# Down projection of seven pairs of token tiles by Strassen's scheme, with the tokens normalised ahead of gate and up

## The chip, the core and the metric

One core of one Trainium2 chip runs the kernel. Its engines work side by side, each through its own list of instructions: TensorE (PE: matrix products into PSUM; PEld: the loading of the stationary operand), VectorE (DVE), ScalarE (ACT), GpSimd (POOL) and SyncE (SP), which here issues the DMAs. The metric is the device time of one execution in microseconds (us). Traces and the profile's page come from one profiled execution.

## The reference

The input is x, 2048 tokens of 640 values. Two blocks follow each other, both with a layer norm in front and a residual sum behind.

```python
def _A_ref(x, wqkv, w_phi, wo):            # H = 32 heads of Dh = 20
    qkv = ((x @ wqkv).reshape(B, S, 3, H, Dh)).transpose(2, 0, 3, 1, 4)
    q, k, v = qkv[0], qkv[1], qkv[2]
    pq = jnp.einsum("bhsd,hdf->bhsf", q, w_phi)
    pk = jnp.einsum("bhsd,hdf->bhsf", k, w_phi)
    phi_q = jnp.concatenate([_softmax(pq), _softmax(-pq)], axis=-1)
    phi_k = jnp.concatenate([_softmax(pk), _softmax(-pk)], axis=-1)
    kv = jnp.einsum("bhsf,bhsd->bhfd", phi_k, v)
    ...
    return o.transpose(0, 2, 1, 3).reshape(B, S, D) @ wo

def _B_ref(x, w_gate, w_up, w_down):       # F = 1536
    h = (x @ w_gate) * (x @ w_up)
    return h @ w_down

h  = x + _A_ref(_layernorm(x), A_wqkv, A_w_phi, A_wo)
h2 = h + _B_ref(_layernorm(h), B_w_gate, B_w_up, B_w_down)
```

There is no nonlinearity between the norm and the product g * u, so the factor 1/std of a token, which enters both g and u, can be taken out and applied as 1/var after the down product.

## The kernel before

The 2048 tokens are 16 tiles of 128; four tiles make a block (b = 0 to 3), so that each block has 512 tokens. The work is written as units, and a unit's name says what it does to which tile: `k`, `v`, `q` are the projections with their exponentials; `K` and `Q` sum and normalise the features; `A` builds the state kv over all tiles; `n` is the product of the features with kv, `h` the output product of the attention with the residual sum (`watt`), `f b.ft.j` one 128-column slice ft of gate and up for block b (`fu`; block 0 is done in two halves, j = 0 and 2), and `d` and `e` the down product of a tile with the store (`fd`; the last block's four tiles have the name `e` for all but the first instruction).

The order of the instructions on each engine is not found while the program runs. It is a table, `ORDER`, with one string of unit names for each engine: the n-th time that a name stands there, the n-th instruction of that unit on that engine has its place. `Prog.place` walks these five lists, gives out the buffers of the pools (four PSUM buffers `ps` of two banks, two output buffers `outb`, two `gate`, and so on) as they come free by estimated times, and `Prog.finish` adds the waits on semaphores. The estimated times (`t`, `lat`) only decide which buffer is given to whom; each engine carries out its list strictly in order and waits where an operand or a buffer is missing.

The steps that the change touches:

- `watt(t)`: ten products on TensorE, of which the last column gives the mean of the attention's output. DVE adds the token's mean (`mh`, L1009), subtracts it from the sum and writes the residual `x_all` (L1012). The tile is turned by a DMA transpose issued by SP (L475) into `hT`, which gate and up read; tiles 0 and 1 are turned by TensorE. Beside this ACT sums the squares (L571), and POOL makes the variance and its inverse `rs` (L1018, L1020). `rs` is wanted only after the down product.
- `fu`: five matmuls of 512 columns for gate, five for up (256 in the halves of block 0). ACT copies gate out of PSUM (L1033), DVE multiplies it with up and writes `hhT` (L1035), which is the stationary operand of the down product. `hhT` and `hT` are double-buffered over the blocks and lie in the memory of the keys, which in the trace and below gives them the name `phik`; the weights of the down product, `Wd`, lie in that of the values and have the name `vaug`.
- `fd(t)`: 24 matmuls of 320 columns (12 slices of the hidden dimension, two halves of the output). For tiles 0 to 11 ACT scales the result and adds the mean (L1048), POOL adds the residual (L1051), SP stores 160 KB. For the last four tiles ACT adds the mean to the residual beforehand (L1058) and DVE does scaling and sum in one instruction (L1069); the last tile is cut into 512 and 128 columns (L1076), with a store for each.

All matrix products go through one helper, line L578 in the profile.

Of the kernel before, what the change touches and what calls it, by code (L numbers as in the profile page):

```python
# [1170 lines left out]
```

## Time and profile before

| | |
|---|---|
| median of 3 runs | 279.02 us (279.02 to 279.13) |
| profiled execution | 279.5 us, span of the trace 277.6 us |
| TensorE busy | 272.1 us, 98% of the span, granted clock 1.0 |
| DVE, ACT, POOL busy | 167.3, 141.6, 107.8 us |
| down product, 384 matmuls in all | group of 360 with 320 columns that the trace names: 50.4 us |

The chain that ended last is read from the end of the trace backwards: at each step to what released the instruction, or to the one before it on the same engine. A group in the list by lines has its busy time, the mean duration of one instruction, and the idle time before it with what ended that. The duration of a matmul is its time through the array, and matmuls overlap, so that their pace is read from a row of them and not from the mean of one. A few matmuls have no record.

### The profile page before, as it was taken

To read this page: it belongs to the slowest core of one execution; us is meant where nothing else is said; L and a number is where in the kernel's file an instruction comes from. 1 tells how busy PE (TensorE), PEld (TensorE's weight loads), DVE (VectorE), ACT (ScalarE), POOL (GpSimd) and SP (SyncE) were. 2 spreads that over 40 slices of the span, in tenths; PEclk is the share of its full clock that TensorE was granted. 3 is DMA by queue.
4 is the path that set the end of the run, shared out by engine and by line. 5 is a ranking of instruction groups with operands and counts; after the bars stand their busy time and mean duration, and the time that the engine had idled before them with its cause. 6 is when DMAs were issued, how large, how long until landed. Compare 5 with 4: busy or idle time off the path is not lost.

```text
span 277.6 us, 5581 instructions
## 1 busy us (share of the span) xinstructions
PE 272.1 (98%) x2258; PEld 185.0 (67%) x2271; DVE 167.3 (60%) x314; ACT 141.6 (51%) x249; POOL 107.8 (39%) x152
## 2 busy tenths in 40 slices
PE   8999999999999999999999999999999999999995
PEld 8777776777877888877746565565565444457773
DVE  1899999999998888667855652353400223331012
ACT  2469999999586873454354814212623414220330
POOL 5437999999822323302341419002334000100520
PEclk9999999999999999999999999999999999999999
DMA  8997989305575557986656322751130000000112
GB/s 189 285 144 165 147 269 399 143 2 86 139 103 106 92 132 138 300 104 87 124 128 72 59 47 50 151 73 24 24 97 24 24 2 0 0 0 2 71 48 72
DMA packets 67241, 28.60 MB, mean 103 GB/s; under 512 B 57744, under 2 KB 65936, under 8 KB 67216
## 3 DMA queue, kind: packets, MB, share of 16 engines
q1 hardware_dynamic: 66288, 27.90, 46.4%
q10 hardware_dynamic: 928, 0.35, 0.5%
q8 instruction: 18, 0.29, 0.4%
q14 instruction: 7, 0.06, 0.1%
HBM read 11.82 MB, written 2.62 MB: 52 GB/s over the span
## 4 chain that ended last, share of the span: by engine, by line
PE 83%; DVE 7%; POOL 4%; DMA 2%; issue 1%; SPq 1%
PE ps L578 82%; POOL phik L871 3%; DVE ps L846 2%; DMA Wp<-in_A_wqkv_dram 2%; DVE Sq L908 2%; DVE Ssum L868 2%; POOL eq L920 1%; SPq L475 1%; DVE Rk L870 1%; PE ps L486 0%; DVE outb L1076 0%; SPq L471 0%; DVE Phi L958 0%; DVE rq L914 0%; DVE nb L849 0%
## 5 line engine op out<-in xcount | busy, mean ns | idle before, releaser
L578 PE MATMUL ps<-phik,Wgu 128*128 128x512 bf16 (+1 forms) x588 | 106.0, 335 | 0.5
L578 PEld LDWEIGHTS ps<-phik,Wgu 128*128 128x128 bf16 x600 | 58.3, 98 | 42.9 <-DVE phik L1035 0.6
L578 PE MATMUL ps<-Wp,xT 128*128 128x320 bf16 (+1 forms) x480 | 69.6, 299 | 0.2 <-ACT phik L854 0.2
L1035 DVE TENSOR_TENSOR phik<-ps,gate 128x512 bf16<-128x512 f32 (+1 forms) x60 | 34.0, 580 | 55.6 <-PE ps L578 50.0
L1033 ACT ACTIVATE gate<-ps 128x512 bf16<-128x512 f32 (+1 forms) x60 | 30.2, 512 | 66.5 <-PE ps L578 50.9
L578 PE MATMUL ps<-vaug,phik 128*128 128x320 bf16 (+3 forms) x559 | 59.4, 265 | 0.2
L578 PEld LDWEIGHTS ps<-Wp,xT 128*128 128x128 bf16 x480 | 45.5, 98 | 17.7 <-ACT phik L854 0.5
L578 PEld LDWEIGHTS ps<-vaug,phik 128*128 128x128 bf16 x560 | 42.6, 98 | 16.2
L871 POOL TENSOR_TENSOR phik<-phik,Rk 128x1280 bf16<-128x1280 bf16 x16 | 37.5, 2361 | 3.4 <-DVE Rk L870 3.1
L1051 POOL TENSOR_TENSOR outb<-t,x_all 128x640 bf16<-128x640 f32 x12 | 16.7, 1399 | 56.1 <-ACT t L1048 56.1
L1048 ACT ACTIVATE t<-ps,mh,rs 128x640 f32<-128x640 f32 x12 | 10.6, 884 | 34.3 <-PE ps L578 24.8
L846 DVE TENSOR_REDUCE ps<-ps 128x1 f32<-128x640 f32 (+1 forms) x32 | 26.2, 821 | 2.7 <-PE ps L578 2.4
L915 POOL TENSOR_TENSOR rq<-Sq,rq 128x33 f32<-128x33 f32 x16 | 4.1, 256 | 58.4 <-DVE rq L914 52.7
L908 DVE TENSOR_REDUCE Sq<-eq 128x66 f32<-128x1320 bf16 x16 | 24.2, 1514 | 2.8 <-ACT eq L854 2.8
L868 DVE TENSOR_REDUCE Ssum<-phik 128x64 f32<-128x1280 bf16 x16 | 23.5, 1471 | 0.2 <-ACT phik L854 0.2
L920 POOL TENSOR_TENSOR eq<-eq,rq 128x660 bf16<-128x660 bf16 x16 | 20.9, 1306 | 0.9
L854 ACT ACTIVATE eq<-ps,nb,rs 128x300 bf16<-128x300 f32 (+2 forms) x26 | 17.0, 688 | 8.1 <-DVE nb L849 6.6
L571 ACT ACTIVATE junk<-x_all 128x640 bf16<-128x640 bf16 x20 | 14.7, 735 | 4.6 <-DVE x_all L1012 4.6
L854 ACT ACTIVATE eq<-ps,nb,nrs 128x300 bf16<-128x300 f32 (+2 forms) x26 | 16.9, 696 | 0.0
L854 ACT ACTIVATE phik<-ps,nb,rs 128x640 bf16<-128x640 f32 x16 | 14.2, 886 | 2.8 <-DVE nb L849 2.6
L1069 DVE SCALAR_TENSOR_TENSOR outb<-ps,rs,t 128x640 bf16<-128x640 f32 x3 | 2.7, 884 | 20.8 <-PE ps L578 18.0
L1018 POOL TENSOR_SCALAR vpe<-shc 128x1 f32<-128x1 f32 x16 | 3.1, 191 | 30.3 <-ACT junk L571 29.4
(86 smaller groups left out, 247.4 us busy)
## 6 DMA issues: line engine op xcount, KB each, us to landing
x_all<-in_A_x_dram SPq DMA_DIRECT2D x4, 640.0 KB, 5.1
out_dram<-outb SPq DMA_DIRECT2D x15, 160.0 KB, 1.8
Wgu<-in_B_w_gate_dram SPq DMA_DIRECT2D x1, 1920.0 KB, 11.3
Wgu<-in_B_w_up_dram SPq DMA_DIRECT2D x1, 1920.0 KB, 16.1
vaug<-in_B_w_down_dram SPq DMA_DIRECT2D x1, 1920.0 KB, 9.1
Wp<-in_A_wqkv_dram SPq DMA_DIRECT2D x1, 800.0 KB, 5.2
phiqT<-in_A_wqkv_dram SPq DMA_DIRECT2D x1, 800.0 KB, 6.6
Wo<-in_A_wo_dram SPq DMA_DIRECT2D x1, 800.0 KB, 7.0
```

Source lines behind the costliest of these rows:

```text
L571: g.op("ACT", lambda e: e.activation(out=junk[:, v.i, :], in_=in_, func=func, accum_out=acc), rd=rd, wr=wr, use=[v], t=0.73, lat=0.97)
L578: ins = e.matmul(o_, lhsT=l_, rhs=r_, start=s_, stop=p_, skip_group_check=True)
L846: g.op("DVE", lambda e: e.tensor_reduce(out=mx(), in_=src(), axis=AX.XY if len(src().shape) == 3 else AX.X, op=ALU.max, apply_absolute_val ...
L854: g.op("ACT", lambda e, s=s, sc=sc, to=to, of=of: e.activation(out=to(s), in_=of(), func=ACT.Exp, bias=nb[:, i:i + 1], scale=sc[:, t:t + 1 ...
L868: g.op("DVE", lambda e: e.tensor_reduce(out=Ssum[:, vs.i, :], in_=x, axis=AX.X, op=ALU.add), rd=R_phik[t], wr=vs.R, use=[vs], t=1.39, lat=1.5)
L871: g.op("POOL", lambda e: e.tensor_tensor(out=x, in0=x, in1=Rk[:, vr.i, :].unsqueeze(2).to_broadcast([P, 2 * H, DH]), op=ALU.mult), rd=vr.R ...
L908: g.op("DVE", lambda e: e.tensor_reduce(out=Sq[:, vs.i, :].rearrange("p (w g) -> p w g", w=NQ), in_=feat(0, NQ).rearrange("p w (g f) -> p ...
L920: return e.tensor_tensor(out=x, in0=x, in1=rq[:, vr.i, :].rearrange("p (w h) -> p w h", h=HW).unsqueeze(3).to_broadcast([P, NQ, HW, DH]), ...
L1033: g.op("ACT", lambda e: e.activation(out=gate[:, vg.i, 0:P * n], in_=PS[v.i][:, 0, 0:P * n], func=ACT.Copy), rd=[v.R[0]], wr=vg.R, use=[v, ...
L1035: g.op("DVE", lambda e: e.tensor_tensor(out=hhT[:, hb, ft, sl], in0=PS[v.i][:, 1, 0:P * n], in1=gate[:, vg.i, 0:P * n], op=ALU.mult), rd=[ ...
L1048: g.op("ACT", lambda e: e.activation(out=t32[:, v3.i, :].rearrange("p (b n) -> p b n", b=2), in_=PS[v.i][:, :, 0:HALF], func=ACT.Identity, ...
L1051: g.op("POOL", lambda e: e.tensor_tensor(out=outb[:, vo.i, :], in0=t32[:, v3.i, :], in1=x_all[:, t, :], op=ALU.add), rd=v3.R + [R_h[t]], w ...
```

## The change

Two things are changed together.

**The down product of a pair of tiles.** The two tiles of a pair are the two block rows of a 2x2 matrix whose block columns are the two halves of the hidden dimension (6 slices of 128 each); `w_down` is cut in the same way into 2x2 blocks of 768 x 320. Strassen's scheme computes the four blocks of the product from seven block products instead of eight, each of sums or differences of blocks. `weight_sums` makes the five sums of weight blocks (T0 to T4, 1920 values a partition) once, on POOL, in the memory of the projection weights `Wp` and of `xT`, which are no longer needed by then. `block_sums` makes the five sums of hidden blocks of a pair (S0 to S4, 768 values a partition) on DVE, in the memory of `xT`. `down_pair` has seven groups of six matmuls. Products that go into two results are copied out of PSUM by ACT as float32 (`snap`, L1161) while further products are added onto them in PSUM; POOL forms the sums of these copies and of the residual (`padd`, L1167, six a pair); DVE adds a sum to what stands in PSUM and writes the output tile (`fin`, L1172, four a pair). A pair takes two of the four PSUM buffers from its first product on. Tiles 0 and 1 (`RAW`) are multiplied as before (`down_raw`).

**The norm ahead of gate and up.** Since sums of two tiles' hidden blocks are formed, both must carry their own 1/std already. For tiles 2 to 15 `watt` now lets ACT sum the squares of h - mean, POOL take the power -1/2, and DVE write the normalised tile `hb` (L1062); the DMA transpose reads `hb`. Nothing has to be scaled after the down product. For tiles 0 and 1 the path stays.

The table `ORDER` is a new one from q2 on, on all engines. On SP two loads of x (`lx2`, `lx1`) stand ahead of the first transposes of the queries, and the load of `w_down` (`ld`) ahead of those of tile 4.

```diff
@@ -42,6 +42,7 @@
 SC = 175.0 / 128.0
+RAW = (0, 1)
...
-        "f3.0.0 f3.0.0 f2.1.0 f3.1.0 f3.11.0 f3.10.0 f3.11.0 f3.1.0 f2.5.0 f2.5.0 e12 d9 e12 d11 d8 e14 d10 e14 e13 e13 e15 e15",
+        "D3.0 D2.1 D3.0 D2.1 D2.1 D3.0 D3.0 D3.0 D3.1 D3.0 D3.1 D3.0 D3.1 D3.1 D3.1 D3.1 D3.1",
...
-    t32 = sb([P, 2, D], FP32, "t32")
+    t32 = sb([P, 2, HALF], FP32, "t32")
+    hb = sb([P, 2, D], BF16, "hb")
...
+    KH = NF // 2
+    xTf = xT[:, :, :, :].rearrange("p t c n -> p (t c n)")
+    eqf = eq[:, :, :].rearrange("p b n -> p (b n)").bitcast(FP32)
+    Wkv = Wp[:, :, D:3 * D]
+    TW = [Wkv[:, 0:3, 0:2 * HALF], Wkv[:, 0:3, 2 * HALF:4 * HALF], Wkv[:, 3:5, 0:3 * HALF],
+          xTf[:, 0:KH * HALF].rearrange("p (a n) -> p a n", a=3), xTf[:, KH * HALF:2 * KH * HALF].rearrange("p (a n) -> p a n", a=3)]
+    o1 = 2 * KH * HALF
+    SH = [[xTf[:, o1 + KH * P * (2 * k + i):o1 + KH * P * (2 * k + i + 1)].rearrange("p (f n) -> p f n", f=KH) for i in range(2)]
+          for k in range(5)]
...
-        g.op("DVE", lambda e: e.tensor_tensor(out=mh[:, t:t + 1], in0=PS[v.i][:, 1, HALF:HALF + 1], in1=mv[:, t:t + 1], op=ALU.add),
-             rd=v.R + [R_mv[t]], wr=[R_mh[t]], use=[v], t=0.11, lat=0.2)
+        if t in RAW:
...
         xv = x_all[:, t, :].rearrange("p (b n) -> p b n", b=2)
+        g.op("DVE", lambda e: e.tensor_tensor(out=xv, in0=PS[v.i][:, :, 0:HALF], in1=xv, op=ALU.add),
+             rd=v.R + [R_x[t // 4]], wr=[R_h[t]], use=[v], t=0.75, lat=0.87)
+        act_sum(x_all[:, t, :], ACT.Square, shc[:, t:t + 1], [R_h[t], R_nmh[t]], [R_shc[t]], bias=nmh[:, t:t + 1])
...
+        vh = Buf(p_hb)
+        g.op("DVE", lambda e: e.tensor_scalar(out=hb[:, vh.i, :], in0=x_all[:, t, :], scalar1=nmh[:, t:t + 1], scalar2=rs[:, i:i + 1],
+                                              op0=ALU.add, op1=ALU.mult), rd=[R_h[t], R_nmh[t], R_rs[i]], wr=vh.R, use=[vh],
+             t=0.27, lat=0.37)
+        turned(t, 1, lambda: hT[:, bb, :, P * tt:P * (tt + 1)], lambda: hb[:, vh.i, :], vh.R, [R_hT[bb][tt]], [vh])
...
+    def weight_sums():
+        lo, hi = (0, HALF), (HALF, D)
+        for k, (a, b, op) in enumerate(((0, 3, ALU.add), (1, 3, ALU.subtract), (2, 0, ALU.subtract), (0, 1, ALU.add), (2, 3, ALU.add))):
+            U("T%d" % k)
+
+            def part(q, n):
+                f0, (c0, c1) = KH * (q // 2), (lo, hi)[q % 2]
+                return Wd[:, f0:f0 + KH, c0:c1].rearrange("p (a w) n -> p a w n", w=n)
+
+            def out_(n, k=k):
+                return TW[k].rearrange("p a (w n) -> p a w n", w=n)
+            n = TW[k].shape[2] // HALF
+            pool_op(lambda e, a=a, b=b, op=op, n=n, part=part, out_=out_: e.tensor_tensor(out=out_(n), in0=part(a, n), in1=part(b, n), op=op),
+                    4.0, rd=[R_Wd], wr=[R_T[k]])
+
+    def block_sums(b, i):
+        hb_, c0 = b % 2, 2 * P * i
+
+        def part(q):
+            f0, c = KH * (q % 2), c0 + P * (q // 2)
+            return hhT[:, hb_, f0:f0 + KH, c:c + P]
+        for k, (x, y, op) in enumerate(((0, 3, ALU.add), (2, 3, ALU.add), (0, 1, ALU.add), (2, 0, ALU.subtract), (1, 3, ALU.subtract))):
+            U("S%d.%d.%d" % (b, i, k))
+            rd = [R_hhT[hb_][ft][2 * i + q // 2] for q in (x, y) for ft in range(KH * (q % 2), KH * (q % 2) + KH)]
+            g.op("DVE", lambda e, k=k, x=x, y=y, op=op: e.tensor_tensor(out=SH[k][i], in0=part(x), in1=part(y), op=op),
+                 rd=rd, wr=[R_S[k][i]], t=0.6, lat=0.72)
...
+        def mm(v, bk, l_, r_, first, more=()):
+            g.op("PE", lambda e: mms(e, [(PS[v.i][:, bk, 0:HALF], l_[0](ft), r_[0](ft), first and ft == 0, False) for ft in range(KH)]),
+                 rd=l_[1] + r_[1], wr=[v.R[bk]], use=[v] + list(more), t=0.815, lat=0.965)
+
+        def slot(x):
+            return eqf[:, HALF * x.i:HALF * (x.i + 1)] if x.i < 6 else t32[:, x.i - 6, :]
+
+        def snap(v, bk):
+            x = Buf(p_slot)
+            o = g.op("ACT", lambda e: e.activation(out=slot(x), in_=PS[v.i][:, bk, 0:HALF], func=ACT.Copy), rd=[v.R[bk]], wr=x.R,
+                     use=[v, x], after=SLOT_USERS, t=0.42, lat=0.55)
+            return x, o
+
+        def padd(o_, a, y, op=ALU.add, x=None):
+            r_, in1 = (y.R, lambda: slot(y)) if x is None else ([R_h[x[0]]], lambda: x_all[:, x[0], HALF * x[1]:HALF * (x[1] + 1)])
+            g.op("POOL", lambda e: e.tensor_tensor(out=slot(o_), in0=slot(a), in1=in1(), op=op), rd=a.R + r_, wr=o_.R,
+                 use=[o_, a] + ([y] if x is None else []), t=0.72)
+
+        def fin(v, bk, o_, t, y=None, after=()):
+            in1 = (lambda: slot(y)) if y is not None else (lambda: x_all[:, t, HALF * bk:HALF * (bk + 1)])
+            g.op("DVE", lambda e: e.tensor_tensor(out=outb[:, o_.i, HALF * bk:HALF * (bk + 1)], in0=PS[v.i][:, bk, 0:HALF], in1=in1(),
+                                                  op=ALU.add), rd=[v.R[bk], R_h[t]] + (y.R if y is not None else []), wr=[o_.R[bk]],
+                 use=[v, o_] + ([y] if y is not None else []), after=after, t=0.45, lat=0.57)
...
+        mm(v1, 1, summed(2), wraw(3), True, [v2])
+        s5, _ = snap(v1, 1)
+        mm(v2, 0, raw(3), wsum_(2), True)
+        s4, _ = snap(v2, 0)
+        mm(v1, 0, summed(0), wsum_(0), True)
+        s1, _ = snap(v1, 0)
+        mm(v1, 1, raw(0), wsum_(1), False)
+        c12, a12 = snap(v1, 1)
+        fin(v1, 1, o1_, t1, after=[a12])
+        mm(v2, 0, summed(1), wraw(0), False)
+        c21, a21 = snap(v2, 0)
+        fin(v2, 0, o2_, t2, after=[a21])
+        mm(v1, 0, summed(4), wsum_(4), False)
+        mm(v2, 1, summed(3), wsum_(3), True)
+        padd(s4, s4, s5, ALU.subtract)
+        padd(s5, s4, None, x=(t1, 0))
+        padd(s1, s1, s4)
+        padd(s1, s1, None, x=(t2, 1))
+        padd(s1, s1, c12)
+        padd(s1, s1, c21, ALU.subtract)
+        fin(v1, 0, o1_, t1, s5)
+        store(o1_, t1)
+        fin(v2, 1, o2_, t2, s1)
+        store(o2_, t2)
...
+    def down(b):
+        for i in range(2):
+            if 4 * b + 2 * i in RAW:
+                down_raw(4 * b + 2 * i)
+                down_raw(4 * b + 2 * i + 1)
+                continue
+            block_sums(b, i)
+            down_pair(b, i)
+
+    for b in range(2):
+        each(queries, b)
+        each(num, b)
+        each(watt, b)
+    each(queries, 2)
+    each(num, 2)
+    each(queries, 3)
+    g.alias(R_T, R_Wp[1] + R_Wp[2] + R_xT[0:6])
+    weight_sums()
+    g.alias([r for x in R_S for r in x], R_xT[5:])
+    ffn(0)
+    each(watt, 2)
+    each(num, 3)
+    ffn(1)
+    down(0)
+    ffn(2)
+    each(watt, 3)
+    down(1)
+    ffn(3)
+    down(2)
+    down(3)
```

What the new order is at three places follows. A row is a source line, operation, output and inputs by name, the shape, and the number of equal instructions in a row.

The end of TensorE's list: before, tiles 13 to 15, each 24 matmuls, the last tile in two parts.

```order
L578 MATMUL ps1<-vaug,phik 128x320 x24
L578 MATMUL ps0<-vaug,phik 128x320 x12
L578 MATMUL ps3<-vaug,phik 128x320 x24
L578 MATMUL ps0<-vaug,phik 128x320 x12
L578 MATMUL ps2<-vaug,phik 128x320 x24
L578 MATMUL ps1<-vaug,phik 128x512 x12
L578 MATMUL ps1<-vaug,phik 128x128 x12
```

In the change, the last two pairs; `xT` and `Wp` are the places of the sums (S, T3 and T4 in `xT`, T0 to T2 in `Wp`).

```order
L604 MATMUL ps0<-xT 128x320 x6
L604 MATMUL ps1<-vaug,xT 128x320 x6
L604 MATMUL ps2<-xT 128x320 x6
L604 MATMUL ps3<-vaug,xT 128x320 x6
L604 MATMUL ps1<-Wp,phik 128x320 x6
L604 MATMUL ps3<-xT 128x320 x6
L604 MATMUL ps2<-Wp,xT 128x320 x6
L604 MATMUL ps2<-Wp,phik 128x320 x6
L604 MATMUL ps1<-vaug,xT 128x320 x6
L604 MATMUL ps2<-xT 128x320 x6
L604 MATMUL ps1<-xT 128x320 x6
```

Three tiles' products have become groups of six that alternate between the pairs, each pair with two PSUM buffers, and the last product is added onto a buffer of which ACT has taken a copy.

The end of POOL's list: before, the residual sums of the last tiles that POOL serves (8 to 11).

```order
L1018 TENSOR_SCALAR vpe<-shc 128x1
L1020 TENSOR_TENSOR rs<-vpe,mone 128x1
L1051 TENSOR_TENSOR outb<-t32,x_all 128x640 x4
```

In the change, the six float32 sums of the last pair, of which the last is wanted for the last output.

```order
L1167 TENSOR_TENSOR t32<-t32,eq 128x320 x2
L1167 TENSOR_TENSOR eq<-eq,t32 128x320
L1167 TENSOR_TENSOR t32<-eq,x_all 128x320
L1167 TENSOR_TENSOR eq<-eq 128x320
L1167 TENSOR_TENSOR eq<-eq,x_all 128x320
L1167 TENSOR_TENSOR eq<-eq 128x320 x2
```

POOL had no part in the last four tiles; now it stands between their products and their outputs.

DVE ahead of block 2 of gate and up: before, the residual of a tile (`x_all`) is what the transpose reads.

```order
L1009 TENSOR_TENSOR mh<-ps3,mv 128x1
L1012 SCALAR_TENSOR_TENSOR x_all<-ps3,mh,x_all 128x640
L1035 TENSOR_TENSOR phik<-ps2,gate 128x512
L993 RECIPROCAL rden<-ps3 128x32
L1035 TENSOR_TENSOR phik<-ps0,gate 128x512
L995 TENSOR_TENSOR ob<-ps3,rden 128x640
```

In the change, the scaled tiles 8 and 9 (the two rows that write `hb`), around the eviction of tile 0's down product.

```order
L1019 RECIPROCAL rden<-ps0 128x32
L1021 TENSOR_TENSOR ob<-ps0,rden 128x640
L1062 TENSOR_SCALAR hb<-x_all,nmh,rs 128x640
L1125 SCALAR_TENSOR_TENSOR outb<-ps1,rs,x_all 128x640
L1062 TENSOR_SCALAR hb<-x_all,nmh,rs 128x640
L1110 TENSOR_TENSOR xT<-phik 128x768
L1019 RECIPROCAL rden<-ps0 128x32
```

The scaling is a further instruction between the residual sum and the transpose, and it has a place of its own in DVE's list, behind an attention tile (`ob`) and a down tile (`outb`).

More of the change, by code (lines that the diff above doesn't have):

```diff
@@ L230, in place @@
                 o = queue[e][head[e]]
-                if any(b.i is None and not b.pool.free for b in o.bufs):
+                want = {}
+                for b in o.bufs:
+                    if b.i is None:
+                        want[b.pool] = want.get(b.pool, 0) + 1
+                if any(len(p.free) < n for p, n in want.items()):
                     continue
@@ L418, in _build @@
     shc = sb([P, NT], FP32, "shc")
[L419 removed]
+    nmh = sb([P, NT], FP32, "nmh")
     mhalf = sb([P, 1], FP32, "mhalf")
@@ L452, in _build @@
     p_Ss, p_Rk, p_Sq, p_rq, p_rden = Pool(2), Pool(2), Pool(2), Pool(2), Pool(2)
+    p_hb, p_slot = Pool(2), Pool(8)
+    R_T, R_S = regs(5), [regs(2) for _ in range(5)]
+    SLOT_USERS = []
     R_x, R_h = regs(4), regs(NT)
@@ L1015, in watt @@
-        turned(t, 1, lambda: hT[:, bb, :, P * tt:P * (tt + 1)], lambda: x_all[:, t, :], [R_h[t]], [R_hT[bb][tt]], [])
-        act_sum(x_all[:, t, :], ACT.Square, shc[:, t:t + 1], [R_h[t]], [R_shc[t]])
+        if t in RAW:
+            g.op("DVE", lambda e: e.tensor_tensor(out=nmh[:, t:t + 1], in0=mv[:, t:t + 1], in1=PS[v.i][:, 1, HALF:HALF + 1], op=ALU.subtract),
+                 rd=v.R + [R_mv[t]], wr=[R_nmh[t]], use=[v], t=0.11, lat=0.2)
+            xv = x_all[:, t, :].rearrange("p (b n) -> p b n", b=2)
+            g.op("DVE", lambda e: e.scalar_tensor_tensor(out=xv, in0=PS[v.i][:, :, 0:HALF], scalar=nmh[:, t:t + 1], in1=xv,
+                                                         op0=ALU.subtract, op1=ALU.add),
+                 rd=v.R + [R_x[t // 4], R_nmh[t]], wr=[R_h[t]], use=[v], t=0.8, lat=0.92)
+            turned(t, 1, lambda: hT[:, bb, :, P * tt:P * (tt + 1)], lambda: x_all[:, t, :], [R_h[t]], [R_hT[bb][tt]], [])
+            act_sum(x_all[:, t, :], ACT.Square, shc[:, t:t + 1], [R_h[t]], [R_shc[t]])
+            i = NT + t
+            pool_op(lambda e: e.tensor_scalar(out=vpe[:, i:i + 1], in0=shc[:, t:t + 1], scalar1=1.0 / D, scalar2=EPS_LN,
+                                              op0=ALU.mult, op1=ALU.add), 0.2, rd=[R_shc[t]], wr=[R_vpe[i]])
+            pool_op(lambda e: e.tensor_tensor(out=rs[:, i:i + 1], in0=vpe[:, i:i + 1], in1=mone[:, 0:1], op=ALU.pow),
+                    0.55, rd=[R_vpe[i], R_const], wr=[R_rs[i]])
+            return
@@ new lines, in down_raw, with two @@
+    def down_raw(t):
+        U("d%d" % t)
+        b, col, i = t // 4, P * (t % 4), NT + t
+        v, vo = Buf(p_ps, 2), Buf(p_outb, 2)
+        g.op("ACT", lambda e: e.activation(out=x_all[:, t, :], in_=x_all[:, t, :], func=ACT.Identity, bias=nmh[:, t:t + 1]),
+             rd=[R_h[t], R_nmh[t]], wr=[R_h[t]], t=0.75, lat=0.83)
+        g.op("PE", lambda e: mms(e, [(PS[v.i][:, bk, 0:HALF], hhT[:, b % 2, ft, col:col + P], Wd[:, ft, HALF * bk:HALF * (bk + 1)],
+                                      ft == 0, ft == NF - 1) for ft in range(NF) for bk in range(2)]),
+             rd=[r[t % 4] for r in R_hhT[b % 2]] + [R_Wd], wr=v.R, use=[v], t=3.257, lat=3.41)
+        def two(x):
+            return x.rearrange("p (b n) -> p b n", b=2)
+        g.op("DVE", lambda e: e.scalar_tensor_tensor(out=two(outb[:, vo.i, :]), in0=PS[v.i][:, :, 0:HALF], scalar=rs[:, i:i + 1],
+                                                     in1=two(x_all[:, t, :]), op0=ALU.mult, op1=ALU.add),
+             rd=v.R + [R_h[t], R_rs[i]], wr=vo.R, use=[v, vo], t=0.8, lat=0.92)
+        g.op("SP", lambda e: e.dma_start(out[0, P * t:P * (t + 1), :], outb[:, vo.i, :]), rd=vo.R, use=[vo], dma=("out", 4),
+             t=0.6, lat=0.3, size=0.4)
@@ L1128, in _build, with each, ffn @@
     load(Wd[:, :, :], B_w_down.rearrange("(f p) n -> p f n", p=P), [R_Wd], 1.92)
-    for b in range(NB):
+    def each(f, b):
         for t in range(4 * b, 4 * b + 4):
-            queries(t)
-        for t in range(4 * b, 4 * b + 4):
-            num(t)
-        for t in range(4 * b, 4 * b + 4):
-            watt(t)
+            f(t)
+    def ffn(b):
         for j, n in SPLIT[b]:
@@ L1138, in _build @@
                 fu(b, ft, j, n)
-        for t in range(4 * b, 4 * b + 4):
-            fd(t)
+    def down(b):
[27 more added lines that the diff above has]
+    down(3)
     g.order = ORDER
```

91 lines of the change are left out of this document (34 added, 57 removed), and 76 rows, old and new, of the table ORDER.

## The prediction

> **What bounds the kernel now.** I read the page's busy times first, then the chain that ended last, then the groups by shape, and the timeline of the end.
>
> ```profile
> span 277.6 us, 5581 instructions
> PE 272.1 (98%) x2258; PEld 185.0 (67%) x2271; DVE 167.3 (60%) x314; ACT 141.6 (51%) x249; POOL 107.8 (39%) x152
> PEclk9999999999999999999999999999999999999999
> PE 83%; DVE 7%; POOL 4%; DMA 2%; issue 1%; SPq 1%
> ...
> 74.88 1.93 PE ps L578 x22
> ...
> 216.60 10.74 PE ps L578 x49
> ...
> 238.18 33.34 PE ps L578 x216
> ...
> 271.57 2.55 PE ps L578 x11
> 274.13 0.03 issue
> 274.15 1.02 DVE outb L1076 x2
> ```
>
> TensorE is busy for 272.1 of 277.6 us at the full granted clock, and from 83 us on the chain consists of its matmuls alone, up to the two evictions that begin at 274.15. Before that, DVE and POOL have a share of the chain (the keys, 40 to 75 us), but TensorE is full there too. So a matmul taken away is time gained, as long as nothing new makes TensorE wait. The 128-column part of the last tile takes another 12 x 0.055 us after 274.13, so TensorE ends at E = 274.8, 2.8 us before the span, and that is half of its 5.5 us of idle time.
>
> **Matmuls removed.** A pair of token tiles has 2x2 blocks of hidden and weights, each block product being 6 matmuls of 320 columns. Eight products become seven in seven pairs: 7 x 6 = 42 of 384 matmuls go.
>
> ```profile
> L578 PE MATMUL ps<-vaug,phik 128*128 128x320 bf16 x360 | 50.4, 299 | 0.1
> ...
> 248.54 7.63 PE L578 MATMUL ps<-vaug,phik 128*128 128x320 bf16 x55
> ...
> 274.93 0.81 SPq L1080 DMA_DIRECT2D out_dram<-outb  x2
> ```
>
> The group gives 50.4/360 = 0.140 us each; 55 in a row take 7.63 us, of which the last one's extra latency is 0.16 (0.299 against 0.14), so 7.47/55 = 0.136. I take 0.136: 42 x 0.136 = **-5.7 us** (-5.9 by the group). The weight loads fall by as many and stay beside the matmuls. One block product is 6 x 0.136 = 0.82 us.
>
> **What the products need.** Prices come from the nearest shapes.
>
> ```profile
> L871 POOL TENSOR_TENSOR phik<-phik,Rk 128x1280 bf16<-128x1280 bf16 x16 | 37.5, 2361 | 3.4 <-DVE Rk L870 3.1 <-DVE nb L849 0.3
> L1035 DVE TENSOR_TENSOR phik<-ps,gate 128x512 bf16<-128x512 f32 x36 | 24.3, 686 | 51.4 <-PE ps L578 47.6 <-ACT gate L1033 3.6
> L1033 ACT ACTIVATE gate<-ps 128x512 bf16<-128x512 f32 x36 | 21.2, 597 | 52.6 <-PE ps L578 38.7 <-DVE phik L1035 12.4 <-DVE x_all L1012 1.5
> L920 POOL TENSOR_TENSOR eq<-eq,rq 128x660 bf16<-128x660 bf16 x16 | 20.9, 1306 | 0.9
> L1051 POOL TENSOR_TENSOR outb<-t,x_all 128x640 bf16<-128x640 f32 x12 | 16.7, 1399 | 56.1 <-ACT t L1048 56.1
> L1048 ACT ACTIVATE t<-ps,mh,rs 128x640 f32<-128x640 f32 x12 | 10.6, 884 | 34.3 <-PE ps L578 24.8 <-DVE outb L1069 7.9 <-POOL outb L1051 1.6
> L1035 DVE TENSOR_TENSOR phik<-ps,gate 128x256 bf16<-128x256 f32 x24 | 9.8, 420 | 4.2 <-PE ps L578 2.4 <-ACT gate L1033 1.4 <-issue 0.2
> L1033 ACT ACTIVATE gate<-ps 128x256 bf16<-128x256 f32 x24 | 9.0, 384 | 13.8 <-PE ps L578 12.1 <-DVE phik L1035 1.7
> ```
>
> - ACT snapshots, 35 of 320 elements: between 384 and 597 ns by width, 0.44 us each, 15 us. Twelve of 884 ns go, so ACT gains little work.
> - DVE final adds, 28 of 320: between 420 and 686, 0.49 us each, 14 us.
> - POOL adds, 42 of 320 with a float32 operand: half of 1399 ns is 0.70; L871 and L920 give a fixed 0.18 us and 1.70 ns an element, which turns 1399 into 0.79 for 320. I take 0.75, 32 us, against 16.7 removed.
> - Block sums S on DVE, 35 of 768 bf16 elements with both inputs in SBUF. No such shape is there. L1035's slope is 1.04 ns an element: upper bound 0.95 us; at half that slope, 0.55. I take 0.6 to 0.95, 21 to 33 us: DVE stays below 220 us of 273.
> - Sign changes of the mean, the bias in the square sum and the residual add without its scalar keep their shapes and durations.
> - Weight sums T on POOL, 5 of 1920: from 0.18 + 1920 x 1.70 ns = 3.4 us to 1920 x 1399/640 = 4.2 us. T2, T1, T0 and T3 stand between the multiplies of queries 11 and 13. POOL needs 14 to 17 us for them and about 5 for the rest up to Q13; TensorE has some 40 us of work between q13 and n13, which waits for it (12 gate/up units of 10 x 0.219 = 2.2 us, the d1 product, three attention outputs and more). They cost nothing with 20 us of cover.
>
> Without their cover each of these would add its sum to the end; the covers are the matmuls of gate/up, which do not change. On SP the two later x loads move ahead of the first query transposes and the w_down load ahead of Q4, h2 and h3.
>
> ```profile
> x_all<-in_A_x_dram SPq DMA_DIRECT2D x4, 640.0 KB, 5.1
> vaug<-in_B_w_down_dram SPq DMA_DIRECT2D x1, 1920.0 KB, 9.1
> ...
> L475 SPq DMA_TRANSPOSE phiqT<-eq x32: 1200/1279/2298, 63.1 to 178.2; - x32
> L475 SPq DMA_TRANSPOSE phik<-x_all x14: 1200/1275/2093, 92.7 to 200.1; - x14
> ```
>
> The first query transposes are issued at 63.1 and n0 runs at about 75, so 5.1 us beside them are covered; the 9.1 us of w_down end before the transposes of h2 are wanted, some 11 us after n3 (7.3 us of products up to h3, then DVE). Zero each, up to 2 us if a transpose queues behind w_down.
>
> **Normalising ahead of gate/up.** For 14 tiles the transpose of h no longer follows the residual add at once: square sum, two POOL steps and the scaling on DVE come in between.
>
> ```profile
> L908 DVE TENSOR_REDUCE Sq<-eq 128x66 f32<-128x1320 bf16 x16 | 24.2, 1514 | 2.8 <-ACT eq L854 2.8
> L846 DVE TENSOR_REDUCE ps<-ps 128x1 f32<-128x640 f32 x26 | 21.2, 819 | 2.6 <-PE ps L578 2.4
> ...
> L571 ACT ACTIVATE junk<-x_all 128x640 bf16<-128x640 bf16 x20 | 14.7, 735 | 4.6 <-DVE x_all L1012 4.6
> L571 ACT ACTIVATION_READ_ACCUMULATOR junk<-x_all 128x1 f32 x20 | 3.9, 196 | 0.0
> L1020 POOL TENSOR_TENSOR rs<-vpe,mone 128x1 f32<-128x1 f32 x16 | 8.7, 551 | 0.7
> L1018 POOL TENSOR_SCALAR vpe<-shc 128x1 f32<-128x1 f32 x16 | 3.1, 191 | 30.3 <-ACT junk L571 29.4
> L1069 DVE SCALAR_TENSOR_TENSOR outb<-ps,rs,t 128x640 bf16<-128x640 f32 x3 | 2.7, 884 | 20.8 <-PE ps L578 18.0 <-DMA out_dram<-outb 2.8
> ...
> L753 DVE TENSOR_SCALAR phiqT<-phiqT,nmeanq x3: 288/377/379, 20.0 to 26.6; 128x640 bf16<-128x640 bf16 x3
> phik<-x_all SPq DMA_TRANSPOSE x14, 2.6
> ```
>
> That is 0.74 + 0.20 + 0.19 + 0.55 + 0.38 = 2.1 us, with hand-overs 2.3, and the places in the queues. The earliest users are the second half of block 0 (f0.6.2), f1.3.0 and f2.7.0. From h3 to f0.6.2 TensorE has eight half units (8 x 1.1), q10, q9 and two small products: 12 us. DVE has about 8 us in front of the scaling of tile 3 (two Sq reductions of 1.51, two adds and the maximum of q10 of 0.82 each, three gate multiplies of 0.42, small ones), then 2.6 us to land: slack about 1.5 to 2.5. For f2.7.0 the scaling of tile 9 stands on DVE behind the eviction of d0 (24 x 0.136 + 0.88 and a hand-over), which ends about 4.3 us after d0's start; with SP's 1.28 and 2.6 us the transpose has landed by 8, and f2.7.0 begins at 10.4: slack 2.4. f1.3.0 begins some 17 us of products after h6, against about 11.5 of DVE work and 2.6 to land: slack 3. No wait is due, but these are the thinnest covers. I book **+0.6 us** for all of them and for the two PSUM buffers that a pair holds, between 0 and 4.
>
> **The end.** The last pair's third product ends four products before TensorE does, at E - 3.3. Snapshot 0.44 and two hand-overs: E - 2.7. Four POOL adds at 0.70 to 0.79: E + 0.1 to E + 0.5. The last add on DVE, 0.49: E + 0.65 to E + 1.05. Before, E is 274.8 and the last eviction ends at 275.17, E + 0.4. The last store is now 160 KB and not 32.
>
> ```profile
> out_dram<-outb SPq DMA_DIRECT2D x15, 160.0 KB, 1.8
> out_dram<-outb SPq DMA_DIRECT2D x1, 32.0 KB, 1.6
> ```
>
> So 0.25 to 0.65 + 0.2, with hand-overs **+0.7 us**. This holds while POOL keeps up: from the last gate/up unit to E there are 24 products, 19.6 us, and about 19 POOL adds, 13 to 15 us. Above 1.0 us an add, POOL sets the end.
>
> **Sum.** -5.7 + 0.6 + 0.7 = -4.4 us. The profiled execution took 279.5 us, span 277.6 and 1.9 around it; the median of the runs is 0.5 lower, 279.02. Taken off all three: span 273.2, profiled 275.1, median **274.6**.
>
> **Rivals.**
> 1. DVE and POOL slow each other in the last 20 us, where ten S sums and the POOL adds run side by side.
>
> ```profile
> L557 DVE TENSOR_TENSOR Phi<-Wrows,G x3: 303/521/537, 6.0 to 6.7; 128x140 bf16<-128x140 bf16 x2, 128x160 bf16<-128x160 bf16 x1
> L557 POOL TENSOR_TENSOR Phi<-Wrows,G x2: 476/504/532, 6.1 to 6.6; 128x140 bf16<-128x140 bf16 x2
> ```
>
> The one place where both read two SBUF inputs: two of DVE's three take 0.52 to 0.54 against 0.30, and POOL's take 0.48 to 0.53 against 0.18 + 140 x 1.70 ns = 0.42. Scaled by 1.75, ten S sums of 0.95 are 16.6 us, and with 16 final adds (7.8) DVE needs 24.4 of 19.6 us: up to +4.8. With sums of 0.55 there is no overrun. The middle of the two, +2.4, gives **277.0**. Chance 0.20. The Trainium skill, SBUF — State Buffer, section "Who interferes with whom", says that a DVE instruction with two SBUF inputs contends with a GpSimd instruction that reads SBUF, and that the later one blocks until the first is done. By that rule ten sums of 0.55 to 0.95 add 5.5 to 9.5 us to POOL's 15 in this stretch, 1 to 5 us more than the 19.6 hold; the rows above show a slowing, but not a full wait.
>
> 2. The longer chain to the transposes is late at f0.6.2, f1.3.0 and f2.7.0. For it: slacks of about 2 us, and L753's 0.38 instead of 0.29 while POOL works. Against: DVE was 60% busy. Overdrawn by 2 us in one place: **276.6**. Chance 0.12.
> 3. Slower: S sums in front of the gate multiplies on DVE hold PSUM. While a pair keeps two of the four buffers, gate/up alternates over two; a buffer must be freed within 2.2 us, the multiply needs 0.76 with its hand-over, so a sum in front of it may take 1.4. With 25 sums in blocks 1 to 3, some of them two in a row, 0.25 us lost at each is 6.2 us: **280.8**. It decides from 0.2 us a sum on, that is where sums take over 1.6 us (0.95 x 1.75). Chance 0.13.
> 4. TensorE's gain shows, but it is as long as before (waits of 4 to 5 us in all): 279. Chance 0.03.
>
> **Chances and range.** My forecast has 0.52, with its own range 273.3 to 275.9 (no new wait; or 1.3 us more). About 0.2% is what a measurement of this kernel tells from no change. Rivals 1 and 2 lie on the faster side, but for a tail of 0.02: faster 0.82, same 0.03, slower 0.15. The range starts at 273.2 and reaches through rivals 1 and 2 to 279.0, which leaves out 0.15 for slower and a few hundredths at either end.
>
> **What would show it.** Right: TensorE's matmuls number 42 fewer, its busy time falls to about 266.5, the chain after 83 us is still matmuls, with gaps below 0.7 us in sum; POOL's add of 320 takes 0.70 to 0.79, S 0.55 to 0.95, T 3.4 to 4.2; TensorE ends 3.5 us before the span. Wrong: TensorE waits for S or for PSUM in the last 25 us (rival 1), for the transposes at the three places (rival 2), or between units of blocks 1 to 3 for DVE's multiply (rival 3). An add beyond 1.0 us or a sum beyond 1.4 would upset the forecast.

## The result: 276.1 us, and a profile that ends on POOL

The changed kernel takes 276.09 us (median of 4 runs, 276.00 to 276.26); the kernel before, measured beside it, 279.07 (median of 4). That is 3.0 us less by the medians; the ratio, formed from all the runs, is 0.9888, 95% interval 0.9871 to 0.9906. The forecast was 274.6, with 4.4 us less. A second measurement, f1 below, gave 0.9892 (0.9877 to 0.9906).

The page of the changed kernel, with span, busy times, granted clock and the shares of the chain that ended last:

```profile
span 274.3 us, 5648 instructions
PE 266.2 (97%) x2217; PEld 181.0 (66%) x2229; DVE 202.0 (74%) x388; ACT 145.9 (53%) x270; POOL 147.9 (54%) x187
PEclk9999999999999999999999999999999999999999
PE 83%; POOL 6%; DVE 4%; DMA 2%; issue 2%; SPq 1%; ACT 1%; POOLq 0%; DVEq 0%
```

TensorE's busy time has fallen from 272.1 to 266.2 us. Its weight loads, of which there is one for each matmul, are 42 fewer (2271 to 2229), as forecast; the matmul records, of which some are missing, went from 2258 to 2217. POOL has 6% of the chain, and the end of the chain shows where (start, duration, what):

```profile
248.43 5.12 PE ps L604 x34
...
253.57 0.45 ACT eq L1161
...
254.09 0.87 POOL eq L1167
...
270.49 0.91 POOLq L371
...
271.49 0.49 DVE outb L1172
```

The snapshot at 253.57 is the second of the third pair from the end, the later of the two that its first add needs. From that add, at 254.09, up to 271.4, the chain is POOL alone: 18 adds (three pairs of six) in 17.3 us, 0.96 us each, one behind the other. The row at 270.49 is the last of them, booked to POOL's queue. TensorE is done before that, as its last row in the timeline of the changed kernel shows:

```profile
267.23 1.80 PE L604 MATMUL ps<-xT 128*128 128x320 bf16 x12
269.59 1.80 POOL L1167 TENSOR_TENSOR eq<-eq 128x320 f32<-128x320 f32 x2
271.49 0.49 DVE L1172 TENSOR_TENSOR outb<-ps,eq 128x320 bf16<-128x320 f32 x1 [2.06 <-POOL eq L1167]
```

TensorE ends at 269.03, POOL 2.4 us after it, and the span 5.3 us after it. Before, that distance was 2.8 us. To see the rest, here are stretches of the span, first of the changed kernel, then of the kernel before (length, then busy time and count of PE, PEld, DVE, ACT, POOL, then clock, DMA share and GB/s):

```profile
85.00:250.00 165.00, 164.37 (x1140) 103.32 (x1150) 109.66 (x207) 71.47 (x150) 68.13 (x83) 1.00 0.37 74
250.00:269.10 19.10, 19.03 (x141) 13.40 (x138) 14.03 (x25) 7.00 (x16) 15.10 (x17) 1.00 0.15 53
```

```profile
85.00:250.00 165.00, 164.34 (x1139) 103.25 (x1149) 86.29 (x154) 69.10 (x138) 39.69 (x62) 1.00 0.40 77
```

Between 85 and 250 us DVE has 23 us more to do and POOL 28, and TensorE is as full as before: 164.37 against 164.34 of 165 us. No new wait has come into this stretch. Up to its end TensorE idles 2.8 us after the change (269.03 less 266.2) and 2.7 before. Nearly all that separates the result from 42 matmuls saved lies behind TensorE's end, in the last 5.3 us.

The prices of the new work, from the groups by shape and from the source views of the adds, of S and of the scaling (duration in ns: minimum/median/maximum):

```profile
L1110 DVE TENSOR_TENSOR xT<-phik 128x768 bf16<-128x768 bf16 x35 | 23.7, 698 | 3.1 <-PE ps L604 3.1
L1098 POOL TENSOR_TENSOR Wp<-vaug 128x1920 bf16<-128x1920 bf16 x3 | 11.7, 3920 | 0.0
L597 ACT ACTIVATE junk<-x_all,nmh 128x640 bf16<-128x640 bf16 x14 | 11.6, 827 | 16.0 <-DVE x_all L1053 15.9
```

```profile
L1167 POOL TENSOR_TENSOR eq<-eq x15: 854/860/1056, 170.4 to 270.5; 128x320 f32<-128x320 f32 x15
L1167 POOL TENSOR_TENSOR eq<-eq,x_all x9: 791/792/990, 171.3 to 268.7; 128x320 f32<-128x320 f32 x9
L1167 POOL TENSOR_TENSOR t<-t,eq x8: 859/862/1176, 203.5 to 265.1; 128x320 f32<-128x320 f32 x8
```

```profile
L1110 DVE TENSOR_TENSOR xT<-phik x35: 546/550/1675, 132.7 to 266.4; 128x768 bf16<-128x768 bf16 x35
L1062 DVE TENSOR_SCALAR hb<-x_all,nmh,rs x14: 338/438/776, 94.9 to 209.7; 128x640 bf16<-128x640 bf16 x14
```

At the median an add of two float32 slots takes 0.86 us and one with the bf16 residual 0.79; the longest takes 1.18. The forecast had 0.75 for both.

### The profile page after: what moved, and what is told of

It is laid out like the page before. It is cut to its first block, busy times and chain, and to the rows that moved or that the text cites. A ratio compares the mean times of both kernels' runs of the same rounds, so it can differ in the third digit from the quotient of the medians.

```text
span 274.3 us, 5648 instructions
## 1 busy us (share of the span) xinstructions
PE 266.2 (97%) x2217; PEld 181.0 (66%) x2229; DVE 202.0 (74%) x388; ACT 145.9 (53%) x270; POOL 147.9 (54%) x187
## 4 chain that ended last, share of the span: by engine, by line
PE 83%; POOL 6%; DVE 4%; DMA 2%; issue 2%; SPq 1%; ACT 1%; POOLq 0%; DVEq 0%
PE ps L604 83%; POOL eq L1167 4%; DMA Wp<-in_A_wqkv_dram 2%; POOL t L1167 2%; DVE ps L872 1%; DVE Sq L934 1%; SPq L501 1%; ACT phik L880 1%; DVE Ssum L894 0%; PE ps L512 0%; DVE Rk L896 0%; POOLq L371 0%; DVE x_all L1039 0%; DVE Phi L984 0%; SPq L497 0%
## 5 line engine op out<-in xcount | busy, mean ns | idle before, releaser
L604 PE MATMUL ps<-phik,Wgu 128*128 128x512 bf16 (+1 forms) x588 | 107.8, 335 | 0.6
L604 PE MATMUL ps<-Wp,xT 128*128 128x320 bf16 (+3 forms) x522 | 76.6, 299 | 0.2 <-ACT phik L880 0.2
L604 PEld LDWEIGHTS ps<-Wp,xT 128*128 128x128 bf16 x522 | 49.8, 98 | 19.5 <-ACT phik L880 0.7
L1167 POOL TENSOR_TENSOR eq<-eq 128x320 f32<-128x320 f32 x15 | 13.2, 881 | 33.1 <-ACT eq L1161 32.6
L1161 ACT ACTIVATE eq<-ps 128x320 f32<-128x320 f32 x27 | 11.8, 438 | 27.0 <-PE ps L604 27.0
L1110 DVE TENSOR_TENSOR xT<-phik 128x768 bf16<-128x768 bf16 x35 | 23.7, 698 | 3.1 <-PE ps L604 3.1
L597 ACT ACTIVATE junk<-x_all,nmh 128x640 bf16<-128x640 bf16 x14 | 11.6, 827 | 16.0 <-DVE x_all L1053 15.9
L604 PE MATMUL ps<-xT 128*128 128x320 bf16 (+1 forms) x144 | 17.4, 266 | 0.0
L604 PEld LDWEIGHTS ps<-xT 128*128 128x128 bf16 x144 | 11.8, 98 | 3.9 <-DVE xT L1110 0.2
```

The lines of the kernel that those rows point to most:

```text
L604: ins = e.matmul(o_, lhsT=l_, rhs=r_, start=s_, stop=p_, skip_group_check=True)
L1110: g.op("DVE", lambda e, k=k, x=x, y=y, op=op: e.tensor_tensor(out=SH[k][i], in0=part(x), in1=part(y), op=op), rd=rd, wr=[R_S[k][i]], t=0.6 ...
L1161: o = g.op("ACT", lambda e: e.activation(out=slot(x), in_=PS[v.i][:, bk, 0:HALF], func=ACT.Copy), rd=[v.R[bk]], wr=x.R, use=[v, x], after= ...
L1167: g.op("POOL", lambda e: e.tensor_tensor(out=slot(o_), in0=slot(a), in1=in1(), op=op), rd=a.R + r_, wr=o_.R, use=[o_, a] + ([y] if x is No ...
```

## The experiments

Two questions are left by the traces. Is it POOL's adds that set the end, and by how much? And are they slow by themselves, or because DVE forms its block sums S beside them? The kernels e1 to e4 ran on one chip beside the kernel before, whose median was 279.39 us there, and f1 to f3 on another, where it was 279.48, against 279.07 in the result. The kernels are therefore compared by their ratios to it; 0.001 is 0.28 us, and the interval of a ratio is 0.3 to 0.5 us to either side. Line numbers shift by a few from kernel to kernel.

**e1, block 3 without its sums.** The ten S of the last two pairs are left out, and their products read plain hidden blocks; the order of everything else stays.

```diff
         def summed(k):
+            if b == 3:
+                return raw((0, 2, 0, 2, 1)[k])
             return lambda ft: SH[k][i][:, ft, :], [R_S[k][i]]
...
-            block_sums(b, i)
+            if b < 3:
+                block_sums(b, i)
             down_pair(b, i)
```

> Block 3's ten sums of hidden blocks (S) are left out: its products read the plain hidden blocks instead, so the last four output tiles are not the reference's. All matmuls, POOL adds, snapshots and final adds stay. In the trace of the change 18 POOL adds run from 254.1 to 271.4 us, and DVE's S sums run beside nine of them. Theory A (POOL sets the end mainly by the length of its adds, 0.86 and 0.79 us alone with 0.08 between two, against the 0.75 that was forecast): only the part above 0.86 goes, some 1.0 us in sum; median about 275.2. Theory B (the end is late mainly because DVE and POOL slow each other): adds fall to 0.75 on average and the tail by 2 us or more; median about 273.9. Theory C (the shortfall is not in the tail): 276.1 as before.

Measured: 274.91 us, ratio 0.9835 (0.9815 to 0.9854), 0.5% or 1.5 us less than the changed kernel. The source view of the adds and the end of the timeline:

```profile
L1168 POOL TENSOR_TENSOR eq<-eq x15: 858/860/942, 171.2 to 269.9; 128x320 f32<-128x320 f32 x15
L1168 POOL TENSOR_TENSOR eq<-eq,x_all x9: 791/792/792, 172.1 to 268.1; 128x320 f32<-128x320 f32 x9
L1168 POOL TENSOR_TENSOR t<-t,eq x8: 859/862/865, 204.3 to 264.6; 128x320 f32<-128x320 f32 x8
```

```profile
254.88 0.86 POOL L1168 TENSOR_TENSOR eq<-eq 128x320 f32<-128x320 f32 x1 [2.33 <-ACT eq L1162]
...
268.02 1.79 PE L603 MATMUL ps<-xT,phik 128*128 128x320 bf16 x12
...
268.97 1.80 POOL L1168 TENSOR_TENSOR eq<-eq 128x320 f32<-128x320 f32 x2
...
270.87 0.49 DVE L1173 TENSOR_TENSOR outb<-ps,eq 128x320 bf16<-128x320 f32 x1 [1.29 <-POOL eq L1168]
```

The long adds of 0.98 to 1.18 us are gone; the median add is as long as it was. The 18 adds run from 254.88 to 270.77: 15.9 us instead of 17.3. So DVE's sums cost POOL 1.4 us. But POOL still ends 1.0 us after TensorE (269.81): with the adds at their plain length, 0.88 us from one to the next, POOL is late too. By the ratio against 279.07 the time is 274.5, between the two theories (275.2 and 273.9), and both hold a part.

**e2, POOL relieved of one add in six.** In the last three pairs DVE adds the residual of the second tile while it takes the first product out of PSUM, in place of ACT's copy and one add of POOL. The order on ACT, DVE and POOL follows that; one S also stands ahead of an eviction on DVE.

```diff
+JOIN = ((2, 1), (3, 0), (3, 1))
...
-        s1, _ = snap(v1, 0)
+        if (b, i) in JOIN:
+            s1 = Buf(p_slot)
+            g.op("DVE", lambda e: e.tensor_tensor(out=slot(s1), in0=PS[v1.i][:, 0, 0:HALF], in1=x_all[:, t2, HALF:D], op=ALU.add),
+                 rd=[v1.R[0], R_h[t2]], wr=s1.R, use=[v1, s1], after=SLOT_USERS, t=0.45, lat=0.57)
+        else:
+            s1, _ = snap(v1, 0)
...
-        padd(s1, s1, None, x=(t2, 1))
+        if (b, i) not in JOIN:
+            padd(s1, s1, None, x=(t2, 1))
```

> For the last three pairs the first product that is taken from PSUM is taken by DVE, which adds the residual in the same instruction, in place of ACT's copy and one of POOL's six adds; nothing else moves but one S sum that goes ahead of an eviction on DVE. The result is the same sum. Theory A: POOL has 15 adds and not 18 in the last stretch and three and not four behind the last copy: POOL ends 2.3 us or more earlier, the last add of DVE then follows TensorE's end (269.0) by 0.1 to 0.2; median 273.7 to 274.1. Theory B: the same adds, still slowed by the S sums, save 0.9 to 1.5; median 274.6 to 275.2. Theory C: 276.1.

Measured: 274.29 us, ratio 0.9815 (0.9799 to 0.9831), 2.1 us below the changed kernel and the fastest kernel here that leaves nothing out. The last pair's adds and the two ends in its timeline:

```profile
264.90 1.19 POOL L1168 TENSOR_TENSOR eq<-eq,t 128x320 f32<-128x320 f32 x1 [0.47 <-ACT eq L1162]
...
267.44 1.79 PE L605 MATMUL ps<-xT 128*128 128x320 bf16 x12
...
269.76 0.49 DVE L1173 TENSOR_TENSOR outb<-ps,eq 128x320 bf16<-128x320 f32 x1 [0.76 <-POOL eq L1168]
```

TensorE ends at 269.23, and the last sum on DVE begins 0.5 us later, not 2.5, though not the 0.1 to 0.2 that theory A expected. POOL's row is no longer unbroken: before the last pair's adds it waits 0.47 us for a copy. By the ratio against 279.07 the time is 273.9, inside what theory A (length and number of the adds) gave. That does not decide between the theories, since an add less also takes one out of DVE's way; f3 bears on what is left.

**e3, the last pair without the scheme.** Tiles 14 and 15 are multiplied plainly from the normalised blocks, 48 matmuls' worth instead of 42, with the last tile cut into 512 and 128 columns and a store for each, as in the kernel before. The other six pairs stay.

```diff
+            if (b, i) == (3, 1):
+                down_norm(14)
+                down_norm(15)
+                continue
             block_sums(b, i)
             down_pair(b, i)
```

> Six pairs by seven products; tiles 14 and 15 get the plain 24 matmuls each, with the residual added by DVE out of PSUM and the last tile in parts of 512 and 128 columns as in the kernel before. TensorE has 6 matmuls more (0.82 us) and ends at 269.9; POOL has 12 adds in the last stretch and ends 5 us before that. Theory A and B (POOL sets the end): the tail is the 2.8 us of the kernel before; span 272.7, median 274.4. Theory C (the shortfall is in the middle): 276.1 + 0.8 = 276.9.

Measured: 274.63 us, ratio 0.9831 (0.9812 to 0.9850), a span of 272.7. The end of its chain:

```profile
82.98 186.37 PE ps L603 x1309
269.34 0.02 issue
269.37 0.96 DVE outb L1224 x2
```

Six matmuls more, and 1.6 us less. The twelve adds that are left end before TensorE does, and the chain from 83 us on is matmuls again. It is the end that lost the time, and not a disturbance of TensorE's matmuls (theory C): with that, six matmuls more would have made the kernel longer.

**e4, the normalisation alone.** Norm ahead of gate and up and the new order as in the change, all tiles multiplied plainly, no T, no S, no adds of POOL.

```diff
-            block_sums(b, i)
-            down_pair(b, i)
+            down_norm(4 * b + 2 * i)
+            down_norm(4 * b + 2 * i + 1)
...
-    weight_sums()
```

> Only the second part of the change: tokens normalised ahead of gate and up, the order of the change, but every tile's down product by 24 plain matmuls, without weight sums, block sums, snapshots and POOL adds; DVE adds the residual out of PSUM. TensorE has the 384 matmuls of the kernel before and the same tail. If the longer chain to the transposes is covered (as the trace of the change has it, with 2.1 us of idle TensorE outside the start and the tail against 1.9 before): 279.0 to 279.4. If the normalisation costs waits in the middle that the change's trace hides in the place of others: 280 to 280.6.

Measured: 279.80 us (10 runs), ratio 1.0014 (1.0005 to 1.0024), which is 0.4 us, between 0.1 and 0.7, more than the kernel before. Against 279.07 that is 279.5, just above the first of the two ranges. The end of the chain, its stretch from 85 to 250 us, and a row of TensorE's waits (us in total, times, longest), first of e4 and then of the changed kernel:

```profile
83.29 191.25 PE ps L597 x1345
274.55 0.02 issue
274.57 0.96 DVE outb L1218 x2
```

```profile
85.00:250.00 165.00, 165.00 (x1158) 103.94 (x1157) 93.90 (x174) 63.94 (x132) 29.40 (x55) 1.00 0.38 74
```

```profile
PE ps L505 <- DVE x_all L1032: 0.4, 1, 0.4
PE ps L512 <- DVE x_all L1039: 0.4, 1, 0.4
```

TensorE waits nowhere between 85 and 250 us, so the longer way to the transposes is covered. (The 0.6 us that the same row of the changed kernel and of the kernel before leaves to 165.00 are gaps of 0.05 us, 12 and 13 of them, as many as their traces have matmuls without a record.) Ahead of that stretch both e4 and the changed kernel have a wait that the kernel before has not: at 82.8 and 82.4 us TensorE waits 0.4 us for the residual of the second of the tiles 0 and 1, which it turns itself. In the new order this stands ahead of ten projections, which before stood in front of it. From 60 to 85 us TensorE is busy 24.33 us in e4 and 24.32 in the changed kernel, against 24.55 before: about half of the 0.4 us. Where the rest lies stays open. Against this kernel the scheme by itself gives 0.9890/1.0014 = 0.9876 (0.9890 is the mean of the two measurements of the changed kernel), 3.5 us of the 5.7 that the matmuls are worth.

**f1, the changed kernel again.** No edit; it is the reference for the next two on their chip.

> The changed kernel, unaltered, once more, beside the next two on one chip. Measured ratio to the kernel before so far: 0.9888 (0.9871 to 0.9906). Both theories expect the same ratio, about 3.0 us less than before, and a tail of 2.4 us between TensorE's end and POOL's last add.

Measured: 276.47 us, ratio 0.9892 (0.9877 to 0.9906), and the same end: 18 adds from 254.92 to 272.21, TensorE's end at 269.86.

```profile
254.92 0.86 POOL L1167 TENSOR_TENSOR eq<-eq 128x320 f32<-128x320 f32 x1 [2.33 <-ACT eq L1161]
...
268.06 1.80 PE L604 MATMUL ps<-xT 128*128 128x320 bf16 x12
...
270.42 1.79 POOL L1167 TENSOR_TENSOR eq<-eq 128x320 f32<-128x320 f32 x2
```

**f2, a dose of two adds.** Each of the last two pairs adds the residual of its first tile once more.

```diff
         padd(s5, s4, None, x=(t1, 0))
+        if b == 3:
+            padd(s5, s5, None, x=(t1, 0))
```

> Each of the last two pairs gets one redundant add of the residual on POOL, behind the first one of that pair (its first tile's output is off by one residual in its first half, so the output is not the reference's). Nothing else moves. Theory A/B, POOL is the bound of the last 17 us without a gap: each add costs its full pitch, 0.79 to 0.99 plus about 0.04 to 0.08 between two, so 1.7 to 2.0 us more than the changed kernel of the same chip. Theory C, the end is set by something else (the last store, the order on DVE, TensorE): 0 to 0.4 us more.

Measured: 277.91 us, ratio 0.9944 (0.9927 to 0.9960), 1.4 us above f1. The first and last POOL rows of its run:

```profile
254.22 0.86 POOL L1167 TENSOR_TENSOR eq<-eq 128x320 f32<-128x320 f32 x1 [2.33 <-ACT eq L1161]
...
271.45 1.79 POOL L1167 TENSOR_TENSOR eq<-eq 128x320 f32<-128x320 f32 x2
```

Twenty adds take 19.0 us, 1.7 more than the 18, as expected; the medians differ by 1.4, a little less than the 1.7 to 2.0, but within what the two intervals leave open (about 0.4 us each). POOL's row is unbroken here too, and it ends later by the time of the two adds: POOL sets the end. The delay also reaches TensorE, whose last products wait 0.7 us for an S that stands on DVE behind a sum of POOL's.

**f3, e2 without the sums of block 3.** Both edits together.

> The kernel e2 (in the last three pairs DVE adds the residual while it takes the first product out of PSUM, so that POOL has five adds a pair), and besides the ten block sums of block 3 left out (its products read plain hidden blocks, so the output is not the reference's). Theory A, only the number and the plain length of POOL's adds mattered: with five a pair POOL is no longer the bound, and the time is that of e2, ratio 0.981 to 0.982. Theory B, what is left between TensorE's end and the last add in e2 is adds that DVE's sums stretch (its last chain begins with one of 1.19 instead of 0.86): 0.3 to 0.5 us less than e2, ratio 0.9797 to 0.9805, with the last eviction within 0.2 us of TensorE's end.

Measured: 273.82 us, ratio 0.9797 (0.9783 to 0.9812), 0.5 us below e2, in the range of theory B. The intervals of the two kernels overlap, so the ratios alone do not decide; the traces do. The two ends:

```profile
267.42 1.79 PE L604 MATMUL ps<-xT,phik 128*128 128x320 bf16 x12
269.40 0.49 DVE L1174 TENSOR_TENSOR outb<-ps,eq 128x320 bf16<-128x320 f32 x1 [0.42 <-POOL eq L1169]
```

TensorE ends at 269.21, and the last sum begins 0.2 us later, against 0.5 in e2. The difference is that of one add, the first of e2's last pair, which takes 1.19 us beside an S and not 0.86. With both causes gone the span ends, at 272.2, 3.0 us after TensorE; the forecast had 3.5, the changed kernel 5.3.

**How the two slow each other.** The rows of DVE and POOL from 254 us on, taken from the timeline of the changed kernel (start, duration):

```profile
254.09 0.86 POOL L1167 TENSOR_TENSOR eq<-eq 128x320 f32<-128x320 f32 x1 [2.33 <-ACT eq L1161]
...
254.39 0.97 DVE L1110 TENSOR_TENSOR xT<-phik 128x768 bf16<-128x768 bf16 x1 [0.20 <-PE ps L604]
...
255.02 0.99 POOL L1167 TENSOR_TENSOR eq<-eq,x_all 128x320 f32<-128x320 f32 x1
...
255.67 0.49 DVE L1172 TENSOR_TENSOR outb<-ps,x_all 128x320 bf16<-128x320 f32 x1 [0.31 <-ACT eq L1161]
255.97 0.85 POOL L1167 TENSOR_TENSOR eq<-eq 128x320 f32<-128x320 f32 x1
...
256.08 2.23 DVE L1110 TENSOR_TENSOR xT<-phik 128x768 bf16<-128x768 bf16 x2
...
256.91 0.99 POOL L1167 TENSOR_TENSOR eq<-eq,x_all 128x320 f32<-128x320 f32 x1
...
257.98 1.06 POOL L1167 TENSOR_TENSOR eq<-eq 128x320 f32<-128x320 f32 x1
```

Alone, S takes 0.55 us, and the add with the residual 0.79. The add that began at 254.09 ends at 254.95. S, begun at 254.39 beside it, ends at 255.36, which is 0.41 after the add's end. The next add, begun at 255.02 beside S, ends at 256.01, which is 0.65 after S's end. Both times the later one has its whole duration less 0.14 us still ahead of it when the earlier one ends.

The next stretch follows the same count: the add of 255.97 ends at 256.82, S 0.41 later at 257.23, the add of 256.91 another 0.65 later at 257.88 (measured 257.90), the second S at 258.31 (measured 258.31), and the add of 257.98, of 0.86, another 0.72 later at 259.03 (measured 259.04). The two engines take turns, and only the first 0.14 us of the waiting instruction lie beside the other.

The final adds of DVE, with one input in PSUM and one in SBUF, do not take part: the one at 255.67, which overlaps two adds, takes 0.49 like the rest. The Trainium skill, SBUF — State Buffer, section "Who interferes with whom", states this as an exclusive lock: a DVE instruction with two SBUF inputs and a reading GpSimd instruction block each other fully, and the one that issues first goes first. The trace agrees, to 0.02 us once those 0.14 us are allowed for.

The count also shows why the lock costs POOL only 1.4 us. Three of block 3's ten sums begin before the 18 adds do; seven run beside them. An add that comes behind such an S loses 0.41 less the usual step of some 0.07 between two adds, less its own 0.14: 0.2 us, and 0.3 where it had begun earlier. Seven adds are hit so, which makes 1.5 us. DVE pays more (0.97 us for one S, 2.23 for the next two), but has time to spare.

Two inputs in SBUF may not be the only case. The scaling `hb` has a single tensor as input, in SBUF, and takes 0.34 to 0.44 us but for one instance, which began 0.2 us into an add, ended 0.19 us after it and took 0.78. No run here tests this further.

```profile
204.46 0.79 POOL L1167 TENSOR_TENSOR eq<-t,x_all 128x320 f32<-128x320 f32 x1
204.66 0.78 DVE L1062 TENSOR_SCALAR hb<-x_all,nmh,rs 128x640 bf16<-128x640 bf16 x1 [2.72 <-DMA phik<-hb]
```

## Why the prediction was nearly right, and where it was not

The direction, the range and the main mechanism held; the gain was 3.0 us and not 4.4. In the terms of the sum:

- **Matmuls, -5.7.** As forecast. TensorE's end went from 274.8 to 269.03 (269.86 in the trace of f1, so that a single trace does not tell tenths), its busy time to 266.2 (forecast about 266.5).
- **New waits in the middle, +0.6.** They came to 0.2 at most: 24.32 against 24.55 us busy from 60 to 85, and 164.37 against 164.34 from 85 to 250. The one new wait, at 82.4 us, is at a place that the forecast did not name. The thin covers of the transposes held (rival 2 is out), and so did PSUM (rival 3 is out: one S reached 1.68 us, beside POOL, which is past the 1.4 named as a sign, but the mean was 0.70). T took 3.9 us at the mean, inside 3.4 to 4.2, without anyone waiting. The square sum with its mean took 0.83 us and not 0.74, and the scaling `hb` 0.44 at the median; both were hidden.
- **The end, +0.7: the step that failed.** It measured +2.5 (2.8 to 5.3 us from TensorE's end to that of the span). The sentence "This holds while POOL keeps up" was the right question with the wrong numbers, in three places. The add was put at 0.75 us; it is 0.86 or 0.79, and 0.88 from one to the next (e1). The time that POOL has was put at 19.6 us from the last gate/up unit for about 19 adds; but the last 18 of them wait for the snapshots and start at 254.09, which leaves 14.9 us up to TensorE's end, or 0.83 an add, so that "above 1.0 us" was too late a limit. And of the lock between DVE and POOL the text says that the rows "show a slowing, but not a full wait"; it is a full wait (but for 0.14 us). The first two put POOL's end 1.0 us after TensorE's, the lock another 1.4.
- **Rival 1** named the mechanism, at 0.20, and gave 277.0. Its sum looked for the overrun on DVE, which has room; it is POOL that overruns. The price, 2.4 us on top, is 1.4. The 5.5 to 9.5 us that it set beside this for ten full waits on POOL were too much as well: seven adds were hit, and an add lost 0.2 to 0.3 us, not the whole of an S.

Span 274.3 against 273.2 forecast: 0.7 us less up to TensorE's end, 1.8 more behind it. The two errors have opposite signs, and that they cancel in part is luck. The other 0.4 us of the 1.5 between 276.1 and 274.6 are no event in the kernel: the profiled execution before lay 0.5 us above its median, that of the change 0.1 below, and the forecast had carried the 0.5 over.
